# Thirty-two repeated columns in the narrow matmuls of a decode kernel

## The chip, the cores and the metric

The kernel runs on one core of a Trainium2 chip. The metric is device time in microseconds (us) of one execution of the whole program; lower is better. The core's engines are TensorE (PE in the profile; its weight loads are listed apart as PEld), VectorE (DVE), ScalarE (ACT), GpSimd (POOL) and SyncE (SP), which here only issues transfers between the chip's memory (HBM) and the on-chip memory (SBUF). TensorE writes to PSUM, eight banks of 128 partitions by 512 fp32 columns. The profile lists the share of its full clock that TensorE was granted (PEclk).

## The reference

Two layers of attention and gated MLP, one token for each of four sequences, all in bf16. Both layers use the same weights and the same caches.

```python
B, Sq, D = 4, 1, 512;  Hq, Hkv, Sk, Dh = 32, 8, 4096, 128;  F = 1792

def A(x, k_cache, v_cache, wq, wo):
    q = (x @ wq).reshape(B, Sq, Hq, Dh).transpose(0, 2, 1, 3)
    k = jnp.repeat(k_cache, 4, axis=1)
    v = jnp.repeat(v_cache, 4, axis=1)
    scores = jnp.einsum("bhqd,bhkd->bhqk", q, k) * (Dh ** -0.5)
    p = softmax(scores)
    o = jnp.einsum("bhqk,bhkd->bhqd", p, v)
    return o.transpose(0, 2, 1, 3).reshape(B, Sq, Hq * Dh) @ wo

def B_(x, w_gate, w_up, w_down):
    return (sigmoid(x @ w_gate) * (x @ w_up)) @ w_down

for layer in range(2):
    x = x + A(layernorm(x), A_k_cache, A_v_cache, A_wq, A_wo)
    x = x + B_(layernorm(x), B_w_gate, B_w_up, B_w_down)
```

One sequence and one KV head have a K and a V of 4096 x 128, 1 MB each; there are 32 such pairs, read in each layer. Four query heads share a KV head.

## The kernel before

**Units.** A layer has 32 units (one sequence, one KV head). `ORDER` lists pairs of units, 32 pairs over both layers, and the main loop (from L1343) takes one pair at a time: scores, softmax and transpose of pair `sg`, and in the same round the product with V of the pair before it, `vg`.

**Transfers.** SBUF has twelve slots of 1 MB and, after the last use of the query weights, four more in their place. `pump` (L441) issues the next K, V or weight load, in the fixed order of `LOADS`, as soon as a slot is free, all from the SP queue. A slot is free when the matmuls that read it (scores L996, product with V L1154) are done, so a late matmul holds up the load that is to reuse its slot and, in the queue, all loads behind it. `RET` names units whose K or V stays in its slot from layer 0 to layer 1.

**A pair.** VectorE transposes K in its slot in 32 x 32 blocks (`k_turn`, L981). `scores` (L983) issues, for each unit, four rounds of four matmuls; the four of a round have a stationary tile of 128 x 32 each, go to four different strips of 32 columns of the array, and stream 256 columns. The softmax is one row maximum on VectorE, one exponential on ScalarE, and small matmuls that spread the maximum (L1042) and sum the parts (L1090). `ptrans` (L1107) turns P with two matmuls that stream 128 columns (L1112), and 16 copies on ScalarE and VectorE take it to SBUF (L1137, L1131).

**Product with V** (`pv`, L1141; `pv_last`, L1171, for the last pair). V is the stationary operand: for each unit 32 matmuls, each with a 128 x 128 tile of V as weights, stream the 4 columns of P that belong to the four query heads and add into 4 columns of the PSUM bank `O_ps[p]`. `normalise` (L1207) multiplies the 8 columns of a pair by the reciprocal sums.

**Output projection** (`wo_mm`, L1221): 32 matmuls with 128 x 128 tiles of `wo` as weights and 1 or 2 columns (one or two sequences) each, into columns 64 to 71 of the same bank; `wo_add` (L1245) adds them to the residual `xT`.

**A pass.** When all units of a sequence in layer 0 are done, its MLP and its next queries run as 23 steps (`pass_steps`, L943), spread over the rounds of the main loop by the table `PLACES`: layer norm (`ln_a`, `ln_b`), gate and up (`wide`, through `wide_mm`, L798: 56 matmuls each, one streamed column), `gate_tanh`, `gate_mul`, `down` (L918: 56 matmuls, one column) and `down_add`; then a second layer norm and `q_row` (L868), which has one column of weights and streams 512 columns of the query weights, four matmuls at a time in four strips; last `q_turn` and `q_spread`. There are four passes, one for each sequence. Each engine works through its instructions in program order, so the steps of a pass stand in TensorE's queue between the matmuls of the pairs.

**The tail** (from L1460) is the MLP of layer 1 for all four sequences at once: gate and up with 4 streamed columns (`wide_mm` again, 56 matmuls each), then `down_rows` (L1484), which has the hidden state as weights (128 x 32 tiles in four strips) and streams 128 columns of `w_down`.

The weights of gate, up, down, output projection and V are all 128 x 128 tiles that are used once each. Each matmul is preceded by a load of its tile (PEld).

Of the kernel before, what the change touches and what calls it, by code (L numbers as in the profile page):

```python
# [6 lines left out]
ACTF = mybir.ActivationFunctionType  # L7
ALU = mybir.AluOpType
# [236 lines left out]
def bass_interleave_layers__gqa_block_cached__glu_gated_glu__decode_kernel(  # L245
# [12 lines left out]
    Bn, Sq, D = A_x.shape  # L258
    _, HKV, SK, DH = A_k_cache.shape
    HQ = A_wq.shape[1] // DH  # L260
    REP = HQ // HKV
    F = B_w_gate.shape[1]
    P = 128
    assert Sq == 1 and DH == P and D == 512 and F % P == 0 and SK == 4096
    assert REP == 4 and Bn == 4 and HKV == 8
    KD = D // P
    KF = F // P
    NJ = SK // P
    XJ = 4
    JG = NJ // XJ  # L270
    NT4 = 4
    NLAYER = 2
    NSLOT = 12
    eps = 1e-5
# [46 lines left out]
    xT = sbt([P, KD, Bn], dt.float32, "xT")  # L321
# [3 lines left out]
    lnsum, _, vpe, nt_a, nt_b, nt_c, nt_y, rs = [newt[:, i, :] for i in range(8)]  # L325
    y0i = newt[:, 8, :].bitcast(dt.int32)
    xc_bf = sbt([P, KD, Bn], dt.bfloat16, "xc_bf")
# [23 lines left out]
    O_ps = [pst("O_ps0"), pst("O_ps1")]  # L351
# [223 lines left out]
    def head_masks():  # L575
# [44 lines left out]
            writes=["blk"],  # L620
        )

    def bsl(b0, nb):
        return slice(b0, b0 + nb)

# [172 lines left out]
    def wide_mm(nb, which, f0, f1, M, mk):  # L798
        wsb, keys = ((wg_sb, wkeys["wg"]), (wu_sb, wkeys["wu"]))[which]
        fns = []  # L800
        for fc in range(f0, f1):
            for k in range(KD):
                fns.append(
                    (lambda fc, k: lambda e: e.matmul(  # L804
                        M[:, 64 + fc * nb:64 + (fc + 1) * nb],
                        lhsT=wsb[:, k, bass.ds(2 * P * (fc // 2) + fc % 2, P, step=2)],
                        rhs=xc_bf[:, k, 0:nb],
                        start=(k == 0),
                        stop=(k == KD - 1),
                    ))(fc, k)  # L810
                )
        S.group("pe", fns, reads=["xcb"] + keys, writes=[mk])

    def tail_tanh():
        dve(
            lambda e: e.tensor_tensor(
                gs_sb.rearrange("p (k b) -> p k b", k=KF),
                M_ps[0][:, 64:64 + KF * Bn].rearrange("p (k b) -> p k b", k=KF),
                bc(rs[:, 0:Bn], KF, Bn),
                ALU.mult,  # L820
            ),
            reads=["M0", "rs"],
            writes=["pe0"],
        )
        act(
            lambda e: e.activation(t_sb, gs_sb, ACTF.Tanh),
            reads=["pe0"],
            writes=["pe0"],
        )

    def tail_mul(h, f0, f1, M, mk, hk):
        dve(
            lambda e: e.scalar_tensor_tensor(
                out=h[:, f0:f1, :],
                in0=t_sb.rearrange("p (k b) -> p k b", k=KF)[:, f0:f1, :],
                scalar=-1.0,
                in1=M[:, 64 + f0 * Bn:64 + f1 * Bn].rearrange("p (k b) -> p k b", b=Bn),
                op0=ALU.add,
                op1=ALU.mult,
            ),  # L840
            reads=["pe0", mk, "h_w"],
            writes=[hk],
        )
# [7 lines left out]

    def gate_tanh():
        act(
            lambda e: e.activation(th, M_ps[0][:, 64:64 + KF], ACTF.Tanh, scale=rs[:, 0:1]),
            reads=["rs", "M0"],
            writes=["xc"],
        )

    def gate_mul():
        dve(  # L860
            lambda e: e.scalar_tensor_tensor(
                out=hT_bf[:, :, 0], in0=th, scalar=-1.0, in1=M_ps[1][:, 64:64 + KF], op0=ALU.add, op1=ALU.mult
            ),
            reads=["xc", "M1"],
            writes=["qT"],
        )
# [51 lines left out]
    def down(nb, c0):  # L918
        fns = []
        for c in range(c0, c0 + 2):  # L920
            for k in range(KF):
                fns.append(
                    (lambda c, k: lambda e: e.matmul(  # L923
                        M_ps[0][:, 128 + c * nb:128 + (c + 1) * nb],
                        lhsT=wd_sb[:, k, bass.ds(2 * P * (c // 2) + c % 2, P, step=2)],
                        rhs=hT_bf[:, k, 0:nb],
                        start=(k == 0),
                        stop=(k == KF - 1),
                    ))(c, k)
                )  # L930
        S.group("pe", fns, reads=["qT"] + wkeys["wd"], writes=["M0"])

    def down_add(b):
        dve(
            lambda e: e.scalar_tensor_tensor(
                out=xT[:, :, b], in0=M_ps[0][:, 128:128 + KD], scalar=rs[:, 0:1], in1=xT[:, :, b],
                op0=ALU.mult, op1=ALU.add,
            ),
            reads=["M0", "rs"],
            writes=[f"x{b}"],  # L940
        )
# [200 lines left out]
    def pv(i):  # L1142
        l, b, u = seq[i]
        g, ul = divmod(i, 2)
        p = g % 2
        s = where["v", b, u]
        pT = pT_sb[p]
        vv = slot[s].rearrange("p (j d) -> p j d", d=DH)
        for x in range(XJ):
            fns = []  # L1150
            for c in range(4):
                for j in range(2):
                    fns.append(
                        (lambda x, c, j: lambda e: e.matmul(  # L1154
                            O_ps[p][:, ul * REP:(ul + 1) * REP],
                            lhsT=vv[:, x * JG + c * 2 + j, :],
                            rhs=pT[:, x, j, 2 * c + ul, :],
                            start=(x == 0 and c == 0 and j == 0),
                            stop=(x == XJ - 1 and c == 3 and j == 1),
                        ))(x, c, j)  # L1160
                    )
            key = f"pT_{x}"
            rd = [f"s{s}", key] + [f"{key}_{a}" for a in range(3)]
            if ul == 0 and x == 0:
                S.group("pe", fns, reads=rd, writes=[f"O{p}"])
            else:
                S.last_write[f"O{p}"] = S.group("pe", fns, reads=rd)
        if l == 1 or not kept("v", i):
            free.append(where.pop(("v", b, u)))

    def pv_last(g):  # L1171
        p = g % 2
        l, b, u = seq[2 * g]
        ss = [where.pop(("v", b, u + ul)) for ul in range(2)]
        pT = pT_last.rearrange("p (j n a h) -> p j n a h", j=2, a=4, h=REP)
        for ul in range(2):
            vv = slot[ss[ul]].rearrange("p (a s j d) -> p a s j d", a=4, s=4, j=2)
            for a in range(4):
                fns = []
                for s in range(4):  # L1180
                    for j in range(2):
                        fns.append(
                            (lambda ul, vv, a, s, j: lambda e: e.matmul(  # L1183
                                O_ps[p][:, ul * REP:(ul + 1) * REP],
                                lhsT=vv[:, a, s, j, :],
                                rhs=pT[:, j, 2 * s + ul, a, :],
                                start=(a == 0 and s == 0 and j == 0),
                                stop=(a == 3 and s == 3 and j == 1),
                            ))(ul, vv, a, s, j)
                        )  # L1190
                rd = [f"v{ul}_{a}", "q0", "q1"]
                if ul == 0 and a == 0:
                    S.group("pe", fns, reads=rd, writes=[f"O{p}"])
                else:
                    S.last_write[f"O{p}"] = S.group("pe", fns, reads=rd)
        free.extend(ss)
# [10 lines left out]
    def normalise(g):  # L1207
        l, b, u = seq[2 * g]
        p = g % 2
        n, c = oplace(l, b)  # L1210
        assert (n, u, c) not in held, (l, b, u)
        held[n, u, c] = (l, b)
        dve(
            lambda e: e.tensor_tensor(  # L1214
                oT_sb[n][:, u * REP:(u + 2) * REP, c], O_ps[p][:, 0:2 * REP], rden_sb[p], ALU.mult
            ),
            reads=[f"O{p}", f"rden{p}"],
            writes=[f"oT{n}_{u}_{c}"],
        )

    def wo_mm(g, p):  # L1221
# [8 lines left out]
        for c in range(KD):  # L1230
            for r in range(2 * REP):
                fns.append(
                    (lambda c, r: lambda e: e.matmul(  # L1233
                        O_ps[p][:, 64 + 2 * c:64 + 2 * c + nb],
                        lhsT=wo_sb[:, u * REP + r, bass.ds(2 * P * (c // 2) + c % 2, P, step=2)],
                        rhs=oT_sb[n][:, u * REP + r, 0:nb],
                        start=(r == 0),
                        stop=(r == 2 * REP - 1),
                    ))(c, r)
                )  # L1240
# [4 lines left out]
    def wo_add(g, p):  # L1245
# [5 lines left out]
        xs = xT[:, :, bass.ds(b0, nb, step=max(1, b1 - b0))]  # L1251
        dve(
            lambda e: e.tensor_tensor(
                xs, xs, O_ps[p][:, 64:64 + 2 * KD].rearrange("p (k two) -> p k two", two=2)[:, :, 0:nb], ALU.add
            ),
            reads=[f"x{b0}", f"x{b1}", f"O{p}"],
            writes=[f"x{b0}", f"x{b1}"],
# [318 lines left out]
```

## Time and profile before

| | |
|---|---|
| median of 3 runs | 311.92 us (311.75, 311.92, 314.68) |
| span of the profiled execution | 310.4 us |
| median less span | 1.5 us |
| read from HBM | 115.61 MB |
| matmuls | 5268, of which 1984 in L1154, 640 in L1233, 560 in L804, 224 in L923, 64 in L1183 |
| matmuls of the scores (L996) | 1024 |
| matmuls of `q_row` (L874) | 128 |

The total time of the profiled execution is not listed beside its span; the 1.5 us between the span and the median are taken as what lies around it. A matmul counts as busy from its issue until its result is in PSUM. Matmuls overlap, and busy time counts overlapping ones once, so a busy PE had work in flight; how much of its rate that used is not said. In rows of stretches, the columns are: from and to, length, busy us and count for PE, PEld, DVE, ACT and POOL, then the granted share of TensorE's clock, the share of the 16 DMA engines, and GB/s. Rows of one source line have PE and PEld alone. In rows of a timeline the first two numbers are start and length.

### The profile page before, as it was taken

Reading aid. Unit: us, or ns where it says so; the run is one execution under the profiler, and the core shown is the slowest. Engines: PE = TensorE matmul, PEld = TensorE weight load, DVE = VectorE, ACT = ScalarE, POOL = GpSimd, SP = SyncE. Lnnn points to the kernel's source line nnn. Section 1 sums busy time; section 2 is a strip of 40 time slices with the busy share of each in tenths; the row PEclk is TensorE's granted clock in tenths of the full one; section 3 lists DMA queues with packets and bytes.
Section 4 is the critical chain, followed back from the end, with each engine's and each line's share of the span. In section 5 each row is a group of like instructions: output and inputs, shape, how many; then the busy total and the mean of one; then the engine's idle time right before and its main releaser. Section 6 shows DMA issues by size and latency. Waiting matters only on the chain. (4 is left out here: it accounts for less than half of the span.)

```text
span 310.4 us, 12244 instructions
## 1 busy us (share of the span) xinstructions
PE 231.6 (75%) x5268; PEld 160.9 (52%) x5268; DVE 205.9 (66%) x597; ACT 118.9 (38%) x489; POOL 26.0 (8%) x106
## 2 busy tenths in 40 slices
PE   1373565676878967589998684889777869988786
PEld 0331113345664645467756462775555658476586
DVE  4654768988646448875854967576888358458823
ACT  1040241345511544325246655513266542545510
POOL 0000000000000100000011000000110000011200
PEclk9999999995555555555557555556555555557555
DMA  7999999999999999999999999999999998999900
GB/s 294 414 400 414 414 421 420 420 419 417 414 405 353 343 414 423 417 420 367 357 358 354 424 422 420 419 378 390 396 422 419 383 423 290 377 387 424 344 18 3
DMA packets 19169, 116.39 MB, mean 375 GB/s; under 512 B 1960, under 2 KB 1964, under 8 KB 6444
## 3 DMA queue, kind: packets, MB, share of 16 engines
q1 hardware_dynamic: 19116, 115.62, 92.8%
q8 instruction: 41, 0.67, 0.8%
q14 instruction: 12, 0.10, 0.1%
HBM read 115.61 MB, written 0.00 MB: 372 GB/s over the span
## 5 line engine op out<-in xcount | busy, mean ns | idle before, releaser
L981 DVE STREAM_TRANSPOSE slot<-slot 128x1024 f32<-128x1024 f32 (+1 forms) x57 | 98.0, 1726 | 10.5 <-DMA slot<-in_A_k_cache_dram 10.4
L1137 ACT ACTIVATE pT<-PT 32x64 bf16<-32x64 f32 x388 | 83.4, 215 | 40.1 <-PE PT L1112 30.4
L996 PE MATMUL S_ps<-slot,qz 128*32 128x256 bf16 x976 | 61.3, 407 | 22.3 <-DVE slot L981 20.5
L1154 PE MATMUL O_ps<-pT,slot 128*128 128x4 bf16 x1952 | 62.9, 166 | 13.2 <-ACT pT L1137 5.9
L1154 PEld LDWEIGHTS O_ps<-pT,slot 128*128 128x128 bf16 x1952 | 58.2, 104 | 22.0 <-ACT pT L1137 9.8
L996 PEld LDWEIGHTS S_ps<-slot,qz 128*32 128x32 bf16 x976 | 28.7, 128 | 38.0 <-DVE slot L981 20.7
L1067 ACT ACTIVATE pe<-S_ps,small 128x256 bf16<-128x256 f32 x32 | 15.5, 485 | 79.5 <-DVE small L1055 55.0
L1081 POOL TENSOR_TENSOR small<-small 128x1 f32<-128x1 f32 x64 | 12.5, 195 | 240.6 <-ACT pe L1067 238.1
L1131 DVE CAST pT<-PT 32x64 bf16<-32x64 f32 x108 | 24.0, 222 | 6.1 <-PE PT L1112 2.9
L1233 PE MATMUL O_ps<-oT,wo 128*128 128x2 bf16 (+1 forms) x640 | 20.1, 165 | 2.2 <-DVE oT L1214 1.9
L1233 PEld LDWEIGHTS O_ps<-oT,wo 128*128 128x128 bf16 x640 | 18.9, 104 | 4.4 <-DVE oT L1214 4.3
L561 ACT ACTIVATE wo<-M_ps 128x512 bf16<-128x512 f32 x14 | 8.3, 594 | 31.9 <-PE M_ps L551 31.8
L1019 DVE TENSOR_REDUCE small<-S_ps 128x1 f32<-128x256 f32 x32 | 13.2, 411 | 6.7 <-PE S_ps L996 6.4
L551 PE MATMUL M_ps<-wo,row 64*128 64x512 bf16 x56 | 14.1, 599 | 4.1 <-DVE wo L566 2.6
L1214 DVE TENSOR_TENSOR oT<-O_ps,rden 128x8 bf16<-128x8 f32 x32 | 5.0, 155 | 16.5 <-PE O_ps L1154 13.6
L874 PE MATMUL M_ps<-wq,xc_bf 128*1 128x512 bf16 x128 | 15.3, 594 | 0.5
L1112 PE MATMUL PT<-ident_bf,pe 128*128 128x128 bf16 x64 | 12.0, 290 | 4.8 <-ACT pe L1067 4.7
L788 POOL TENSOR_TENSOR qz<-qc,small 128x128 bf16<-128x128 bf16 x32 | 12.6, 401 | 28.9 <-ACT qc L774 28.9
L1042 PE MATMUL MS<-row_max,mask_f 128*128 128x16 bf16 x64 | 6.9, 181 | 10.5 <-DVE row_max L1025 10.5
L566 DVE CAST wo<-M_ps 128x512 bf16<-128x512 f32 x14 | 9.6, 683 | 6.5 <-PE M_ps L551 6.4
L1055 DVE CUSTOM_DVE_ANT_0 junk<-MS,small 128x16 bf16<-128x16 f32 x32 | 6.8, 212 | 9.5 <-PE MS L1042 9.4
L1042 PEld LDWEIGHTS MS<-row_max,mask_f 128*128 128x128 bf16 x64 | 4.1, 107 | 16.6 <-DVE row_max L1025 13.6
(104 smaller groups left out, 205.4 us busy)
## 6 DMA issues: line engine op xcount, KB each, us to landing
slot<-in_A_v_cache_dram SPq DMA_DIRECT2D x49, 1024.0 KB, 10.4
slot<-in_A_k_cache_dram SPq DMA_DIRECT2D x42, 1024.0 KB, 10.2
wq<-in_A_wq_dram SPq DMA_DIRECT2D x4, 1024.0 KB, 7.8
wo<-in_A_wo_dram SPq DMA_DIRECT2D x8, 512.0 KB, 14.4
wq<-in_A_k_cache_dram SPq DMA_DIRECT2D x3, 1024.0 KB, 11.8
slot<-in_A_v_cache_dram SPq DMA_DIRECT2D x8, 256.0 KB, 16.5
wg<-in_B_w_gate_dram SPq DMA_DIRECT2D x2, 896.0 KB, 18.3
wu<-in_B_w_up_dram SPq DMA_DIRECT2D x2, 896.0 KB, 9.9
```

The source lines that it names most:

```text
L551: (lambda h, i, rows: lambda e: e.matmul(ps[h][:, :], lhsT=spread_w[i][rows, :], rhs=wo_sb[rows, c + i, :], start=(i == 0), stop=(i == 1), ...
L788: lambda e: e.tensor_tensor(qz_sb[z][:, :, 0:4 * REP].rearrange("p i (a r) -> p i a r", r=REP), qc_sb[:, b, u:u + 2, :, :].rearrange("p u ...
L874: (lambda k, st: lambda e: e.matmul(M_ps[h][32 * st:32 * st + 1, :], lhsT=xc_bf[:, k, 0:1], rhs=wv[:, k, h, :, st, :], start=(k == 0), sto ...
L981: dve(lambda e: e.transpose(kf, kf), writes=[f"s{st}"])
L996: (lambda t, b2, e_, w0, s: lambda e: e.matmul(S_ps[p][32 * s:32 * s + 8 * REP, 0:2 * P], lhsT=qzf[:, w0:w0 + 8 * REP], rhs=ktv[:, :, s, : ...
L1019: lambda e: e.tensor_reduce(m, S_ps[p][:, 0:2 * P], AX.X, ALU.max),
L1067: lambda e: e.activation(to, frm, ACTF.Exp, bias=nm_sb[p], scale=exp_scale, accum_out=sm_sb[p][0],),
L1081: (lambda n: lambda e: e.tensor_tensor(sm_sb[p][n + 1], sm_sb[p][n], top(sm_sb[p][n]), ALU.subtract))(n),
L1131: (lambda dst, frm: lambda e: e.tensor_copy(dst, frm))(dst, frm),
L1137: (lambda dst, frm: lambda e: e.activation(dst, frm, ACTF.Copy))(dst, frm),
L1154: (lambda x, c, j: lambda e: e.matmul(O_ps[p][:, ul * REP:(ul + 1) * REP], lhsT=vv[:, x * JG + c * 2 + j, :], rhs=pT[:, x, j, 2 * c + ul, ...
L1233: (lambda c, r: lambda e: e.matmul(O_ps[p][:, 64 + 2 * c:64 + 2 * c + nb], lhsT=wo_sb[:, u * REP + r, bass.ds(2 * P * (c // 2) + c % 2, P, ...
```

## The change

The matmuls of five functions get their right-hand operand repeated, so that each streams 32 columns: `wide_in` reads the same 1, 2 or 4 columns 32, 16 or 8 times (a stride of zero, no copy is made), and `wide_out` gives the result 32 columns of PSUM in place of 1, 2 or 4. Every repeat computes the same numbers. `wide_cols` picks the first 1, 2 or 4 of each 32 for the readers. The weights, the number of matmuls and of weight loads, their order, the semaphores and the transfers are as they were. The places in PSUM move: product with V to columns 0 to 63, output projection to 64 to 191, gate and up to 64 to 511, down to 128 to 255 of their banks, and the instructions of VectorE and ScalarE that read them now step by 32 columns.

```diff
+    WIDE = 32
...
+    def wide_in(ap):
+        n = ap.shape[1]
+        return ap.unsqueeze(1).broadcast_to([P, WIDE // n, n])
+
+    def wide_out(M, i, n):
+        return M[:, WIDE * i:WIDE * (i + 1)].rearrange("p (w n) -> p w n", n=n)
+
+    def wide_cols(M, i, k, n):
+        return M[:, WIDE * i:WIDE * (i + k)].rearrange("p (k w) -> p k w", w=WIDE)[:, :, 0:n]
...
# wide_mm (gate and up)
-                        M[:, 64 + fc * nb:64 + (fc + 1) * nb],
+                        wide_out(M, 2 + fc, nb),
                         lhsT=wsb[:, k, bass.ds(2 * P * (fc // 2) + fc % 2, P, step=2)],
-                        rhs=xc_bf[:, k, 0:nb],
+                        rhs=wide_in(xc_bf[:, k, 0:nb]),
...
# gate_tanh
-            lambda e: e.activation(th, M_ps[0][:, 64:64 + KF], ACTF.Tanh, scale=rs[:, 0:1]),
+            lambda e: e.activation(th, wide_cols(M_ps[0], 2, KF, 1)[:, :, 0], ACTF.Tanh, scale=rs[:, 0:1]),
...
# down
-                        M_ps[0][:, 128 + c * nb:128 + (c + 1) * nb],
+                        wide_out(M_ps[0], 4 + c, nb),
                         lhsT=wd_sb[:, k, bass.ds(2 * P * (c // 2) + c % 2, P, step=2)],
-                        rhs=hT_bf[:, k, 0:nb],
+                        rhs=wide_in(hT_bf[:, k, 0:nb]),
...
# pv (pv_last in the same way)
-                            O_ps[p][:, ul * REP:(ul + 1) * REP],
+                            wide_out(O_ps[p], ul, REP),
                             lhsT=vv[:, x * JG + c * 2 + j, :],
-                            rhs=pT[:, x, j, 2 * c + ul, :],
+                            rhs=wide_in(pT[:, x, j, 2 * c + ul, :]),
...
# normalise
-                oT_sb[n][:, u * REP:(u + 2) * REP, c], O_ps[p][:, 0:2 * REP], rden_sb[p], ALU.mult
+                oT_sb[n][:, u * REP:(u + 2) * REP, c].rearrange("p (t r) -> p t r", t=2),
+                wide_cols(O_ps[p], 0, 2, REP),
+                rden_sb[p].rearrange("p (t r) -> p t r", t=2),
+                ALU.mult,
...
# wo_mm
-                        O_ps[p][:, 64 + 2 * c:64 + 2 * c + nb],
+                        wide_out(O_ps[p], 2 + c, nb),
                         lhsT=wo_sb[:, u * REP + r, bass.ds(2 * P * (c // 2) + c % 2, P, step=2)],
-                        rhs=oT_sb[n][:, u * REP + r, 0:nb],
+                        rhs=wide_in(oT_sb[n][:, u * REP + r, 0:nb]),
...
```

The other readers (`tail_tanh`, `tail_mul`, `gate_mul`, `down_add`, `wo_add`) change in the way of `gate_tanh`. The scores, `q_row`, `ptrans`, the layer norms and `down_rows` are not touched.

More of the change, by code (lines that the diff above doesn't have):

```diff
@@ L817, in tail_tanh @@
                 gs_sb.rearrange("p (k b) -> p k b", k=KF),
-                M_ps[0][:, 64:64 + KF * Bn].rearrange("p (k b) -> p k b", k=KF),
+                wide_cols(M_ps[0], 2, KF, Bn),
                 bc(rs[:, 0:Bn], KF, Bn),
@@ L836, in tail_mul @@
                 scalar=-1.0,
-                in1=M[:, 64 + f0 * Bn:64 + f1 * Bn].rearrange("p (k b) -> p k b", b=Bn),
+                in1=wide_cols(M, 2 + f0, f1 - f0, Bn),
                 op0=ALU.add,
@@ L861, in gate_mul @@
             lambda e: e.scalar_tensor_tensor(
-                out=hT_bf[:, :, 0], in0=th, scalar=-1.0, in1=M_ps[1][:, 64:64 + KF], op0=ALU.add, op1=ALU.mult
+                out=hT_bf[:, :, 0], in0=th, scalar=-1.0, in1=wide_cols(M_ps[1], 2, KF, 1)[:, :, 0],
+                op0=ALU.add, op1=ALU.mult,
             ),
@@ L935, in down_add @@
             lambda e: e.scalar_tensor_tensor(
-                out=xT[:, :, b], in0=M_ps[0][:, 128:128 + KD], scalar=rs[:, 0:1], in1=xT[:, :, b],
+                out=xT[:, :, b], in0=wide_cols(M_ps[0], 4, KD, 1)[:, :, 0], scalar=rs[:, 0:1], in1=xT[:, :, b],
                 op0=ALU.mult, op1=ALU.add,
@@ L1183, in pv_last @@
                             (lambda ul, vv, a, s, j: lambda e: e.matmul(
-                                O_ps[p][:, ul * REP:(ul + 1) * REP],
+                                wide_out(O_ps[p], ul, REP),
                                 lhsT=vv[:, a, s, j, :],
-                                rhs=pT[:, j, 2 * s + ul, a, :],
+                                rhs=wide_in(pT[:, j, 2 * s + ul, a, :]),
                                 start=(a == 0 and s == 0 and j == 0),
@@ L1253, in wo_add @@
             lambda e: e.tensor_tensor(
-                xs, xs, O_ps[p][:, 64:64 + 2 * KD].rearrange("p (k two) -> p k two", two=2)[:, :, 0:nb], ALU.add
+                xs, xs, wide_cols(O_ps[p], 2, KD, nb), ALU.add
             ),
```

## The prediction

> **What bounds the kernel now.** I read the page first: the busy shares, then the slices of clock and transfers.
>
> ```profile
> span 310.4 us, 12244 instructions
> ...
> PE 231.6 (75%) x5268; PEld 160.9 (52%) x5268; DVE 205.9 (66%) x597; ACT 118.9 (38%) x489; POOL 26.0 (8%) x106
> ...
> PEclk9999999995555555555557555556555555557555
> DMA  7999999999999999999999999999999998999900
> GB/s 294 414 400 414 414 421 420 420 419 417 414 405 353 343 414 423 417 420 367 357 358 354 424 422 420 419 378 390 396 422 419 383 423 290 377 387 424 344 18 3
> ```
>
> Transfers bound most of the span: many slices stand at about 421 GB/s. But some fall to 343 to 390, and at the end there are none. The waits of the transfer queue say what it waits for; columns are total us, times, longest.
>
> ```profile
> SPq L237 <- PE O_ps L1154: 108.7, 40, 8.1
> SPq L237 <- PE S_ps L996: 64.2, 21, 6.2
> ```
>
> It waits for matmuls that free a slot. While other transfers are in flight such a wait costs nothing; so I cut out the four stretches in which GB/s fell, which hold the four MLP passes, and the tail.
>
> ```profile
> 80.00:112.00 32.00, 26.00 (x595) 18.42 (x592) 16.33 (x65) 10.56 (x45) 2.92 (x12) 0.50 0.97 377
> 144.00:170.00 26.00, 24.59 (x593) 17.66 (x590) 15.62 (x59) 10.57 (x45) 2.28 (x9) 0.56 0.93 347
> 200.00:224.00 24.00, 20.21 (x502) 14.83 (x501) 17.65 (x60) 6.42 (x26) 1.54 (x6) 0.57 0.99 387
> 256.00:280.00 24.00, 22.75 (x535) 16.09 (x531) 14.88 (x60) 10.07 (x43) 2.28 (x9) 0.50 0.93 354
> 296.00:310.40 14.40, 11.30 (x360) 10.62 (x356) 4.60 (x25) 1.13 (x4) 0.00 (x0) 0.50 0.02 5
> ```
>
> There TensorE is busy 94 of 106 us, at a granted clock of 0.50 to 0.57. Against 421 GB/s the four lose 32(1-377/421)=3.3, 4.6, 1.9 and 3.8 us, 13.7 together: what a faster TensorE could win there at most. The 14.4 us of the tail have no transfers. So the clock matters in 120 of 310 us.
>
> **What moves the clock.** These are stretches of 3.41 us, cut where the granted clock changes or might have changed.
>
> ```profile
> 156.49:159.91 3.42, 3.42 (x58) 1.36 (x50) 1.21 (x8) 1.35 (x4) 0.39 (x2) 0.50 0.96 383
> 159.91:163.32 3.41, 3.06 (x102) 2.71 (x101) 1.95 (x7) 1.07 (x5) 0.76 (x2) 0.50 0.89 320
> ...
> 211.10:214.52 3.42, 3.35 (x43) 0.84 (x35) 2.96 (x16) 1.69 (x9) 0.00 (x0) 0.50 1.01 371
> 214.52:217.93 3.41, 2.82 (x86) 2.02 (x82) 1.86 (x9) 1.15 (x3) 0.39 (x2) 1.00 1.01 423
> ...
> 296.43:299.84 3.41, 3.37 (x128) 3.30 (x124) 0.88 (x4) 0.38 (x1) 0.00 (x0) 0.50 0.02 5
> 299.84:303.26 3.42, 3.10 (x77) 2.80 (x73) 0.94 (x6) 0.51 (x2) 0.00 (x0) 0.50 0.02 5
> ```
>
> All three upper rows of the pairs are full of matmuls, yet only the second is followed by a clock of 1.00, which lasts one such stretch. The timeline shows the difference and, further down, what the clock is worth.
>
> ```profile
> 24.24 1.05 PE L996 MATMUL S_ps<-slot,qz 128*32 128x256 bf16 x16 [2.45 <-DVE slot L981]
> 105.75 0.30 PE L763 MATMUL M_ps<-qT,ident_bf 128*32 128x32 bf16 x16
> 156.23 1.88 PE L874 MATMUL M_ps<-wq,xc_bf 128*1 128x512 bf16 x16
> 159.03 1.02 PE L874 MATMUL M_ps<-wq,xc_bf 128*1 128x512 bf16 x8
> 211.95 2.84 PE L874 MATMUL M_ps<-wq,xc_bf 128*1 128x512 bf16 x24
> 244.12 1.01 PE L1154 MATMUL O_ps<-pT,slot 128*128 128x4 bf16 x32
> 245.00 0.37 PE L1112 MATMUL PT<-ident_bf,pe 128*128 128x128 bf16 x2
> 245.30 1.04 PE L996 MATMUL S_ps<-slot,qz 128*32 128x256 bf16 x16
> 283.37 0.94 PE L1154 MATMUL O_ps<-pT,wq 128*128 128x4 bf16 x32
> 285.19 0.65 PE L996 MATMUL S_ps<-wq,qz 128*32 128x256 bf16 x16 [0.29 <-DVE oT L1214]
> 297.17 1.85 PE L1183 MATMUL O_ps<-slot,slot 128*128 128x4 bf16 x64
> 298.88 2.03 PE L1233 MATMUL O_ps<-oT,wo 128*128 128x2 bf16 x64
> 306.05 1.45 PEld L1489 LDWEIGHTS PT<-wd,slot 128*32 128x32 bf16 x56 [0.15 <-issue]
> 306.08 1.68 PE L1489 MATMUL PT<-wd,slot 128*32 128x128 bf16 x56
> ```
>
> The rate first. L1489 runs 14 rounds of four strips, 128 columns each; less a last matmul of 0.31 us (the form's mean, below) 13 rounds take 1.37 us, 105 ns each: 1.2 columns per ns, or 0.83 ns per column, at clock 0.50. Now the columns streamed. From 211.10: six rounds of 512 (2.56 us) and the end of 16 score matmuls from 210.80, some 0.5 us: about 0.9 of the stretch. From 156.49: 1.45 us left of four rounds, then two, 0.85 us: 0.70. From 296.43: some 95 matmuls of 2 or 4 columns every 27 ns: 0.1. So columns streaming through the array raise the clock and loading weights does not, from a share between 0.70 and 0.9; I take 0.75 as an estimate. One warning: the 1.00 of the first 67 us is no measurement. Sixteen score matmuls take 1.05 us at 24.24, as at 245.30 with 0.50, but 0.65 at 285.19, with a true 1.00. The profile's mean clock is too high by that.
>
> **The change part by part.** Weights, order, waits and transfers stay. Three things change.
>
> First, the added columns. A narrow matmul comes every (1.01-0.17)/31 = 27 ns at clock 0.50, with 0.17 from the first row here.
>
> ```profile
> L1154 PE MATMUL O_ps<-pT,slot 128*128 128x4 bf16 x1952 | 62.9, 166 | 13.2 <-ACT pT L1137 5.9 <-issue 3.9 <-DMA slot<-in_A_v_cache_dram 3.2
> L1489 PE MATMUL PT<-wd,slot 128*32 128x128 bf16 x56 | 1.7, 311 | 0.1
> ```
>
> One or four columns make no difference to it (L1233 with 2: (2.03-0.17)/63 = 30 ns, with a wait in it), so the load of 128 columns sets the 27 ns. The new stream is 32 x 0.83 = 27 ns: it just fits, if load and stream run at once. Rows for that: the two L1112, full tiles with 128 columns, take 0.37 us. One takes 0.17 and 124 more columns of 0.83 ns, 0.27; the second stream adds 0.107: 0.376. Nothing is left for a second load of 27 ns, which would give 0.40. L763, 32 columns behind loads of 32, is the form nearest in size: four rounds in 0.30, less one matmul of some 0.19 (0.17 and 28 columns), leaves 0.11 for three, 37 ns at most, its start included. So 0 to 10 ns more for each narrow matmul; I take 0, by L1112, which has the same full tile. [...]
>
> Second, latency. The last matmul of each group ends 28 columns later, 23 ns at 0.50. Where a pair's work fills the wait it costs nothing. On the chain of a pass there are five such ends (product with V, projection, gate, up, down), and five in the tail: 25 x 0.023 = 0.6 us, taken as if nothing hid it. The readers in PSUM touch as many elements as before, with another step: 0.
>
> Third, the clock. I work it out for the stretch from 144 to 170. Its lines by source, PE and PEld, in this order: L996, L874, L1154, L804, L923, L1233.
>
> ```profile
> 144.00:170.00 26.00, 5.86 (x100) 0.56 0.93 347
> 144.00:170.00 26.00, 3.92 (x32) 0.56 0.93 347
> 144.00:170.00 26.00, 5.88 (x192) 0.56 0.93 347
> 144.00:170.00 26.00, 3.58 (x112) 0.56 0.93 347
> 144.00:170.00 26.00, 1.81 (x56) 0.56 0.93 347
> 144.00:170.00 26.00, 1.35 (x45) 0.56 0.93 347
> ```
>
> Streamed at 0.83 ns per column: scores 25 rounds of 256, 5.3 us; queries 8 rounds of 512, 3.4; the 405 narrow ones about 1. That is 0.37 of 26 us. With 32 columns the narrow ones stream 10.8 us: 0.75. The mean now stands at the threshold, so about half of the 3.41 us stretches should pass it. As the row from 214.52 shows, a rise lasts one stretch when the next streams little (there 82 narrow matmuls and few others). A rise after every second or third stretch makes 0.33 to 0.5 of the time; I take 0.4. Already granted are 0.12 and 0.14 in the second and third stretch, 0.065 on the mean of four: net 0.335.
>
> What full clock saves in that stretch: scores 1.04 to 0.65 for 16, so 6.25 x 0.39 = 2.4 us; queries half of 3.4, 1.7; narrow matmuls (1.01-0.94)/31 = 2 ns each, 405 of them, 0.8. Together 4.9 us in 26, or 0.19 us per us. By the number of matmuls (595+593+502+535 = 2225 against 593) the four stretches would save 18.4 us at full clock, and 18.4 x 0.335 = 6.2 at the share above. How much of that brings transfers forward? None where a slot was free in time; all where the queue stood. TensorE is busy in 0.88 of these stretches, but a saving in front of a wait on VectorE is lost. I take two thirds, 4.1 us, well under the 13.7. The bounds are 0 and 6.2. In the 190 us outside, transfers run at 421 GB/s and cover TensorE: 0.
>
> The tail: the stretch from 296.43 would stream 0.93 instead of 0.1, so the next, from 299.84, has full clock; then one without, then full clock from 306.67, inside L1489, which halves the last 1.1 us of that line: 0.5 saved. For 299.84 to 303.26 I use 0.19 x 3.4 = 0.6. Together 1.1 us.
>
> Sum: -4.1 -1.1 +0.6 = -4.6, a span of 305.8. The median stands 1.5 us above the span: **307.3 us**. With the conversion at 0 it is 311.4, with all of 6.2 it is 305.2.
>
> **The rivals.** *The clock stays up.* The fall after 217.93 came from a stretch with PE busy 2.82 of 3.41 us, but one of mostly narrow matmuls that stream little; wide ones might hold the clock. With a share of 0.8 in the stretches: 18.4 x (0.8-0.065) x 2/3 = 9.0; tail 12 us x 0.19 = 2.3; plus 0.6: a span of 299.7, time 301.2. [...]
>
> *Nothing comes of it.* The clock rises, but the queue is then held by the VectorE chains of the layer norm or the K transposes (DVE busy 17.65 of 24 in the third stretch); or repeats count less than I think. Time 311 to 312.5. For it: shares of 0.75 lie just at the threshold.
>
> *Load and stream do not overlap.* This ends slower. Its place is every narrow matmul of the four stretches and the tail: 2225 x 405/593 = 1520, and 64+64+112 = 240. At 27 ns each it is 47.5 us, a time near 359 with no rise of the clock to set against it, down to 336 if idle time takes half of it. It decides from 4.6/1760 = 2.6 ns per matmul, where it eats the gain; with (4.6+3.1)/1760 = 4.4 ns the kernel is 1% slower. The upper end of 10 ns from L763 would cost 17.6 less 4.6: 325. Against it stands L1112.
>
> *Latency alone*: the clock does not rise, and the ends cost more than 23 ns each because readers queue behind them on in-order engines: 314 to 316.
>
> **Chances.** Forecast 0.50 (own range 304.5 to 310); clock stays up 0.12; nothing 0.22; no overlap 0.10; latency alone 0.06. One per cent, 308.8 and 315.0, is about what a measurement of this kernel tells from no change (three runs spread over 311.75 to 314.68). Of the forecast's half, 0.40 lies below 308.8 and 0.10 above; with 0.12 for a held clock that is 0.52 faster. Same: 0.10, 0.22 and 0.04 of latency, 0.36. Slower: 0.12. The range runs from 301, which takes in the held clock at its worked-out size, to 312.5, which takes in the nothing case. Outside lie the slower two, 0.16, and some 0.04 for a clock that gives more than worked out.
>
> **What would show it.** In the profile after: 32 matmuls of L1154 still in 1.0 us at clock 0.50; granted stretches of 1.00 in each pass and from about 299.8; GB/s over 365 in the four stretches, later ones starting earlier; scores at 0.65 us for 16 in more places. A spacing of 54 ns, or a clock that stays 0.50 while 0.8 of a stretch streams, would prove the first or third step wrong; a risen clock with unchanged GB/s, the conversion.

## The result, and the profile after

| | before | after |
|---|---|---|
| median, first comparison | 311.84 us (4 runs) | 307.89 us (4 runs) |
| ratio, with its 95% interval | | 0.9856 (0.9809 to 0.9903) |
| ratio in two repeats on other occasions | | 0.9912 (0.9883 to 0.9940), 0.9894 (0.9851 to 0.9938) |
| span of the profiled execution | 310.4 us | 306.0 us |

The three intervals together put the gain at about 1%, some 3 us; the forecast was 4.6 us and 307.3 us. The medians of the two repeats were 309.19 beside 311.88 us and 308.80 beside 312.60 us, so the forecast lies a little under all three. The ratios leave out executions in the chip's slower state and the medians do not, so the two can differ by some tenths of a per cent.

The page of the changed kernel, first its span, busy time, granted clock and transfer rate in 40 slices:

```profile
span 306.0 us, 12244 instructions
...
PE 221.0 (72%) x5268; PEld 157.6 (51%) x5268; DVE 206.1 (67%) x597; ACT 118.2 (39%) x489; POOL 25.8 (8%) x106
...
PEclk9999997956655797565799777575965575879567
...
GB/s 289 415 398 413 417 420 419 422 417 420 415 401 356 359 420 423 416 418 391 357 386 381 424 423 417 419 422 388 356 423 420 384 379 347 334 418 420 399 93 3
```

TensorE's busy time fell by 10.6 us though its 3472 narrow matmuls stream 32 columns each; the clock line has many slices over 5 where it had few. Next, the four stretches of the passes, cut at the same times as before (columns as in the prediction):

```profile
80.00:112.00 32.00, 25.84 (x617) 18.91 (x613) 16.54 (x65) 10.59 (x46) 2.75 (x12) 0.66 0.98 384
144.00:170.00 26.00, 20.97 (x603) 16.59 (x602) 18.40 (x60) 11.47 (x49) 2.27 (x9) 0.89 0.98 372
200.00:224.00 24.00, 18.59 (x460) 13.03 (x458) 16.55 (x54) 5.52 (x23) 1.53 (x6) 0.77 0.98 389
256.00:280.00 24.00, 21.47 (x590) 16.57 (x587) 17.15 (x66) 9.75 (x42) 2.26 (x9) 0.80 0.95 369
```

In all four the clock rose. The rates are 377 to 384, 347 to 372, 387 to 389 and 354 to 369 GB/s; against 421 GB/s these four lose 2.8, 3.0, 1.8 and 3.0 us, 10.6 where it was 13.7. Only the second of these differences stands out from what executions differ by: 342 to 351 GB/s in the four runs below that have a clock of at most 0.64 there (places alone, 16 columns, 24 columns, added work), 357 to 377 in the four other traces with 32 columns. In the third and fourth stretch the kernel with the new places alone, nearly at the old clock, has rates above those of the changed kernel:

```profile
200.00:224.00 24.00, 20.16 (x485) 14.08 (x486) 17.52 (x58) 5.75 (x23) 1.53 (x6) 0.57 1.00 409
256.00:280.00 24.00, 22.59 (x538) 15.79 (x537) 15.75 (x63) 9.96 (x42) 2.26 (x9) 0.57 0.98 375
```

Near the end of the loads, both kernels in steps of 2 us, before first:

```profile
292.00:294.00 2.00, 2.00 (x53) 1.45 (x53) 1.58 (x7) 1.41 (x7) 0.00 (x0) 0.50 0.90 326
294.00:296.00 2.00, 0.99 (x34) 0.91 (x33) 0.53 (x4) 0.83 (x2) 0.39 (x2) 0.50 0.29 106
```

```profile
290.00:292.00 2.00, 1.76 (x61) 1.65 (x58) 1.21 (x7) 0.50 (x1) 0.00 (x0) 0.50 0.96 353
292.00:294.00 2.00, 1.95 (x68) 1.85 (x64) 0.67 (x3) 0.72 (x3) 0.39 (x2) 0.50 0.35 128
```

The loads end some 2 us earlier. The timeline gives the rest, each row with its start and length; the first two show the stream's fit, the last two the tail:

```profile
151.54 0.95 PE L1166 MATMUL O_ps<-pT,slot 128*128 128x32 bf16 x32
...
152.77 0.66 PE L1008 MATMUL S_ps<-slot,qz 128*32 128x256 bf16 x16
...
292.59 1.06 PE L1166 MATMUL O_ps<-pT,slot 128*128 128x32 bf16 x32
...
293.57 1.87 PE L1195 MATMUL O_ps<-slot,slot 128*128 128x32 bf16 x64
295.27 1.83 PE L1248 MATMUL O_ps<-oT,wo 128*128 128x32 bf16 x64
```

The last product with V starts at 293.57, where it started at 297.17 before: 3.6 us earlier. From there to the end it is 306.0-293.57 = 12.4 us, before 310.4-297.17 = 13.2: 0.8 us. Together that is the 4.4 us between the spans. Executions of the kernel before lie anywhere from 309.8 to 314.4 us on three occasions, and an experiment below with nearly the old clock has a span of 308.4, so a split read from one execution of each is good to a us or two.

### The profile page after: what moved, and what is told of

It reads as the page before. It is cut to its first block, busy times and chain, and to the rows that moved or that the text cites. A ratio compares the mean times of both kernels' runs of the same rounds, so it can differ in the third digit from the quotient of the medians.

```text
span 306.0 us, 12244 instructions
## 1 busy us (share of the span) xinstructions
PE 221.0 (72%) x5268; PEld 157.6 (51%) x5268; DVE 206.1 (67%) x597; ACT 118.2 (39%) x489; POOL 25.8 (8%) x106
## 5 line engine op out<-in xcount | busy, mean ns | idle before, releaser
L1166 PE MATMUL O_ps<-pT,slot 128*128 128x32 bf16 x1952 | 63.0, 183 | 11.5 <-ACT pT L1149 4.7
L1008 PE MATMUL S_ps<-slot,qz 128*32 128x256 bf16 x976 | 53.4, 363 | 22.6 <-DVE slot L993 19.2
L1166 PEld LDWEIGHTS O_ps<-pT,slot 128*128 128x128 bf16 x1952 | 56.9, 101 | 19.8 <-ACT pT L1149 8.6
L1079 ACT ACTIVATE pe<-S_ps,small 128x256 bf16<-128x256 f32 x32 | 15.5, 484 | 77.0 <-DVE small L1067 34.4
L1008 PEld LDWEIGHTS S_ps<-slot,qz 128*32 128x32 bf16 x976 | 26.0, 116 | 36.0 <-DVE slot L993 19.4
L1093 POOL TENSOR_TENSOR small<-small 128x1 f32<-128x1 f32 x64 | 12.4, 193 | 236.6 <-ACT pe L1079 234.1
L1248 PE MATMUL O_ps<-oT,wo 128*128 128x32 bf16 x640 | 21.3, 187 | 4.6 <-issue 2.2
L1054 PE MATMUL MS<-row_max,mask_f 128*128 128x16 bf16 x64 | 6.9, 178 | 14.8 <-DVE row_max L1037 14.5
L1031 DVE TENSOR_REDUCE small<-S_ps 128x1 f32<-128x256 f32 x32 | 13.2, 411 | 5.0 <-PE S_ps L1008 4.6
L552 PE MATMUL M_ps<-wo,row 64*128 64x512 bf16 x56 | 13.3, 565 | 4.1 <-DVE wo L567 2.6
L1124 PE MATMUL PT<-ident_bf,pe 128*128 128x128 bf16 x64 | 11.1, 270 | 4.3 <-ACT pe L1079 4.1
L886 PE MATMUL M_ps<-wq,xc_bf 128*1 128x512 bf16 x128 | 12.0, 478 | 0.5
```

The costliest lines, as they stand in the source:

```text
L552: (lambda h, i, rows: lambda e: e.matmul(ps[h][:, :], lhsT=spread_w[i][rows, :], rhs=wo_sb[rows, c + i, :], start=(i == 0), stop=(i == 1), ...
L886: (lambda k, st: lambda e: e.matmul(M_ps[h][32 * st:32 * st + 1, :], lhsT=xc_bf[:, k, 0:1], rhs=wv[:, k, h, :, st, :], start=(k == 0), sto ...
L1008: (lambda t, b2, e_, w0, s: lambda e: e.matmul(S_ps[p][32 * s:32 * s + 8 * REP, 0:2 * P], lhsT=qzf[:, w0:w0 + 8 * REP], rhs=ktv[:, :, s, : ...
L1031: lambda e: e.tensor_reduce(m, S_ps[p][:, 0:2 * P], AX.X, ALU.max),
L1079: lambda e: e.activation(to, frm, ACTF.Exp, bias=nm_sb[p], scale=exp_scale, accum_out=sm_sb[p][0],),
L1093: (lambda n: lambda e: e.tensor_tensor(sm_sb[p][n + 1], sm_sb[p][n], top(sm_sb[p][n]), ALU.subtract))(n),
```

## The experiments

**Theory.** Columns that stream through the array raise the granted clock when they fill about three quarters of a stretch of 3.41 us. The share is the prediction's estimate, between a stretch of 0.70 without a rise after it and one of 0.9 with one; the length is that of the trace, for the 8 and 36 clock records of the kernels before and after all start a whole number of 3.41 us from the first of their trace. 32 repeats lift the passes over that mark at next to no cost, because the loads of weights hide them (32 products with V take 1.06 us at half clock from 292.59, 1.01 before); the faster TensorE frees slots sooner (the loads end some 2 us earlier). **Rivals.** The new places in PSUM do it; one part of the matmuls does it alone; any repeat counts; or, the clock being right, more clock would give more. All ratios are against the kernel before, run beside it. The page's mean clock isn't compared between kernels, since all slices ahead of the first recorded change read 9.

**Places alone, 16 columns, 24 columns.** The helpers get a width; the places stay.

```diff
-    def wide_in(ap):
+    def wide_in(ap, w=WIDE):
         n = ap.shape[1]
-        return ap.unsqueeze(1).broadcast_to([P, WIDE // n, n])
+        return ap.unsqueeze(1).broadcast_to([P, w // n, n])
...
# places alone: w = n at every call; 16 and 24 columns: w = 16, w = 24 at every call
```

Expected of the places alone:

> The PSUM places and readers of the changed kernel, but 1 to 4 streamed columns as before. Theory (time comes from the clock, the clock from streamed columns): four single stretches of 3.41 us at full clock as before, mean clock 0.63, time 311.0 to 312.6. Rival (the new places or stepped readers give the gain, or cost something): 308 or over 313 at an unchanged clock.

Expected of 16 columns:

> 16 streamed columns in place of 32, everywhere. Theory: share from 144 to 170 of 0.37 + 0.38/2 = 0.56, below the threshold of about 0.75 in most stretches of 3.41 us, so a mean clock of 0.63 to 0.68 and a time of 310 to 312. Rival (any repeat counts, or matmul busy time counts): clock 0.72 to 0.75 and 307 to 308.5. If the 29 to 31 ns of gate and down come from the stream not quite fitting, they go back to 27.

Expected of 24 columns:

> 24 streamed columns in place of 32. Theory (a threshold near 0.75 of a stretch of 3.41 us): the share from 144 to 170 is 0.37 + 0.75 x 0.38 = 0.66, so more rises than with 16 columns (7) and fewer than with 32 (16 to 18), full clock for 40 to 80 us in all, time between 309.5 and 311.5. Rival (any stream above 16 columns does it): 16 or more rises, 100 us or more, and the time of the changed kernel.

Measured: places alone 0.9994 (0.9968 to 1.0020); 16 columns 1.0018 (0.9990 to 1.0046); 24 columns 0.9972 (0.9937 to 1.0006). The clock line of each page, in this order, one fence for each kernel:

```profile
PEclk9995555555555755555556555555655555575555
```

```profile
PEclk9999999996555575575567555556555555557555
```

```profile
PEclk9999999995555765575578775555755665557556
```

A 5 is half clock. After the leading nines (no record yet) there are 5, 7 and 13 rises in the three traces, 18 in the changed kernel (16 in each of its two repeats); full clock lasts 17, 24 and 48 us, against 106 (109 and 99). So the places and the stepped readers do nothing to the time, 16 columns nothing, and 24 nothing that can be told from none. A threshold would fit that: of the 13 rises that 32 columns add to the 5 of the places alone, half of the columns add 2, and none of the gain. Rises and full clock of 24 columns are as expected. The expected time of 16 columns (310 to 312) was met as a ratio; its median of 313.1 us was not.

**One part alone.** The product with V wide and the rest narrow, and the reverse.

```diff
# product with V alone: in wide_mm, down and wo_mm
-                        wide_out(M, 2 + fc, nb),
+                        wide_out(M, 2 + fc, nb, nb),
...
-                        rhs=wide_in(xc_bf[:, k, 0:nb]),
+                        rhs=wide_in(xc_bf[:, k, 0:nb], nb),
...
# the rest alone: in pv and pv_last
-                            wide_out(O_ps[p], ul, REP),
+                            wide_out(O_ps[p], ul, REP, REP),
```

Expected of the product with V alone:

> 32 columns in the product with V alone; gate, up, down and output projection stream 1 to 4. Theory: from 144 to 170 the streamed share falls from 0.75 to (5.3+3.4+192 x 0.027)/26 = 0.53, so clock there under 0.75 where the changed kernel has 0.89, and in the tail no rise after the output projection; time 309 to 310.5. Rival (the product with V, the most numerous, gives all): 307.5 to 308.5.

Expected of the rest alone:

> 32 columns in gate, up, down and output projection alone; the product with V streams 4. Theory: share from 144 to 170 of (5.3+3.4+0.6+213 x 0.027)/26 = 0.58, clock there under 0.75, outside the passes 0.50; time 309 to 310.5. Rival (only the narrow matmuls of the passes matter, since the transfers cover the rest): 307.5 to 308.5. Spacing of gate and down 29 to 31 ns as in the changed kernel.

Measured: 0.9968 (0.9934 to 1.0002) and 0.9998 (0.9963 to 1.0032), medians 311.85 and 311.70 us beside 311.75. The clocks were as expected, under 0.75 in every stretch; here the second, for V alone and then for the rest:

```profile
144.00:170.00 26.00, 22.43 (x575) 16.16 (x573) 17.42 (x60) 11.53 (x50) 2.26 (x9) 0.68 0.96 351
```

```profile
144.00:170.00 26.00, 24.44 (x616) 18.03 (x609) 16.25 (x61) 11.33 (x49) 2.28 (x9) 0.70 0.96 356
```

The times missed: I expected 309 to 310.5 of both. Neither part gains anything that can be told from none, and the two ratios together would make 0.3%; both at once make 1%. Rates stay at 351 and 356 GB/s at a clock near 0.7, and reach 372 only at 0.89. But the rest alone has 10 rises and 34 us of full clock, and V alone has 16 rises and 78 us, three quarters of the changed kernel's:

```profile
PEclk9995557956555855575569575755757765598575
```

So the sum of full clock does not give the time by itself. In the four stretches V alone has 0.61, 0.68, 0.62 and 0.72; by the prediction's 18.4 us and the conversion found below that would be worth about 1.5 us, which its interval (up to 2.1 us) does not exclude. These runs do not settle whether V alone gains that or nothing.

**No single column repeated.** In the changed kernel a trait showed that I had not forecast: down, with one column repeated 32 times, takes 2.09 us for 56 matmuls at full clock, where the product with V takes 0.95 for 32. Single columns were written 2 or 4 times side by side and those repeated.

```diff
-                out=hT_bf[:, :, 0], in0=th, scalar=-1.0, in1=wide_cols(M_ps[1], 2, KF, 1)[:, :, 0],
+                out=hT_bf[:, :, 0:Bn], in0=th.unsqueeze(2).broadcast_to([P, KF, Bn]), scalar=-1.0, in1=wide_cols(M_ps[1], 2, KF, Bn),
...
-                        rhs=wide_in(hT_bf[:, k, 0:nb]),
+                        rhs=wide_in(hT_bf[:, k, 0:Bn]),
...
# the same for xc_bf (4 copies) and for oT of single sequences (2 copies)
```

Expected:

> The changed kernel with 2 or 4 copies of the one streamed column written side by side, so that no matmul repeats a single column (gate, up, down and projection of single sequences: 928 matmuls, spacing 30 ns against 27 in the product with V, and 30 at full clock against 25). Theory (a column repeated with stride zero is read more slowly): spacing back to 27 at half clock and 25 at full; 928 x 3 to 5 ns = 3 to 4.5 us of TensorE's time, two thirds of it in the end: 2 to 3 us under the changed kernel. Rival (the 30 ns come from the weights' stride of 2 or from the bank): spacing unchanged, time the same as the changed kernel.

Measured: 0.9907 (0.9884 to 0.9930), beside 0.9912 for the changed kernel on the same chip. Down in the timeline, changed kernel and then copies, both at full clock:

```profile
149.61 2.09 PE L935 MATMUL M_ps<-qT,wd 128*128 128x32 bf16 x56
```

```profile
150.03 1.80 PE L936 MATMUL M_ps<-qT,wd 128*128 128x32 bf16 x56
```

Over all starts in the trace the spacing of a repeated single column is 30 to 31 ns at half and at full clock; with copies it is 27.0 to 27.3 and 25.0 to 25.6. With 16 repeats of a single column, in the run above, it was 27.0 to 27.3 at half clock, as 16 columns read at the same slow pace, some 15 ns (an estimate, half of the 30 to 31 for 32), would still fit beside the load's 27 ns. So the theory of the cause holds, and what it should have given, 2 to 3 us, did not come. Once more, beside another run of the changed kernel:

> The changed kernel again, to be compared with the next two on one chip: 0.985 to 0.992 of the kernel before.

> The kernel with side by side copies again. Theory after the first run (what it saves lies where TensorE then waits for VectorE or for transfers): the same as the changed kernel within 1 us. Rival (the 3 us of TensorE's time count by two thirds): 2 us faster than the changed kernel.

Measured: 0.9894 (0.9851 to 0.9938) and 0.9901 (0.9867 to 0.9935), both as expected. The 3 us of TensorE's time are worth nothing that can be measured.

**More clock.** 64 columns in the product with V, the rest as in the changed kernel (the output projection moves on to columns 128 to 255), which ran again beside it and the next.

```diff
+    def pv_in(ap):
+        return ap.unsqueeze(1).broadcast_to([P, 64 // REP, REP])
+
+    def pv_out(M, i):
+        return M[:, 64 * i:64 * (i + 1)].rearrange("p (w n) -> p w n", n=REP)
...
-                            wide_out(O_ps[p], ul, REP),
+                            pv_out(O_ps[p], ul),
...
-                            rhs=wide_in(pT[:, x, j, 2 * c + ul, :]),
+                            rhs=pv_in(pT[:, x, j, 2 * c + ul, :]),
```

Expected of the changed kernel again, and of 64 columns:

> The changed kernel once more, on the chip of the next three, so that they can be compared with it. Theory and rival alike: 0.98 to 0.99 of the kernel before, clock in the four stretches 0.65 to 0.9.

> 64 streamed columns in the product with V, 32 in the rest. Theory: 53 ns spacing at half clock, 27 at full; stretches of product with V always pass the threshold, so a clock of 0.8 to 0.95 in the four stretches; what that wins is set against 1984 x 27 ns x the half-clock share (about 0.25): within 1.5 us of the changed kernel. Rival (a clock that is up nearly always wins more): 301 to 304.

Measured: 0.9912 (0.9883 to 0.9940), just outside what was expected, and 1.0027 (0.9990 to 1.0064). The clock line of 64 columns, and the same product at half clock and at full:

```profile
PEclk9999997979956759976699979669969798999799
```

```profile
95.82 1.87 PE L1172 MATMUL O_ps<-pT,slot 128*128 128x64 bf16 x32
...
156.75 1.09 PE L1172 MATMUL O_ps<-pT,slot 128*128 128x64 bf16 x32
```

Full clock lasted 184 us, the most of all, and the gain is gone: at half clock 32 products take 1.87 us in place of 1.06, and at full clock 1.09 in place of 0.95. My forecast missed too: by the two ratios the kernel is 3.6 us slower than the changed kernel, where I expected 1.5 us at most. The rival that more clock wins more falls, at this price; what so much clock would win without the price is not shown. The run also shows what the forecast's slower rival would have looked like: at half clock the 1.87 us, less a last matmul of some 0.22 (0.17 and 60 columns of 0.83 ns), leave 53 ns for each of 31, the 64 x 0.83 ns of the stream and no longer the 27 ns of the load.

**What TensorE's time is worth.** The kernel before, with 9 more narrow matmuls in each product with V of the main loop.

```diff
+            for c in range(3 if x < XJ - 1 else 0):
+                fns.append(
+                    (lambda x, c: lambda e: e.matmul(
+                        O_ps[p][:, 400:404],
+                        lhsT=vv[:, x * JG + c, :],
+                        rhs=pT[:, x, 0, c, :],
+                        start=False,
+                        stop=False,
+                    ))(x, c)
+                )
```

Expected:

> The kernel before with 9 more narrow matmuls in each product with V (4 columns, into PSUM columns that nobody reads): 558 x 27 ns = 15 us of TensorE's time, 209 of them, 5.6 us, in the four stretches, and no change of the clock. It measures what TensorE's time is worth in the end. Theory (two thirds of the time in the four stretches reaches the end): 3.7 us slower than before. Rival (transfers cover it): within 1 us of before. If all of it counted: 15 us slower.

Measured: 1.0273 (1.0238 to 1.0307), 8.5 us for 15 us of work. That lies between my 3.7 and all of it, and above the theory. Part of the reason is in a stretch that I had counted as covered by transfers, before and then with the added work:

```profile
224.00:256.00 32.00, 24.75 (x574) 17.54 (x578) 22.01 (x52) 17.78 (x80) 3.70 (x15) 0.50 1.01 413
```

```profile
224.00:256.00 32.00, 25.45 (x634) 18.65 (x630) 23.60 (x54) 16.12 (x72) 3.12 (x13) 0.50 0.98 373
```

The cover there is thin: with more work for TensorE the rate fell from 413 to 373 GB/s, though by then the run is 4 to 6 us late, and the stretch holds the end of the third pass as well. Counted by the starts of the same matmuls in both traces, the work of 224 to 256 lost 1.9 us of the 8.8 between the spans. The work of the four stretches lost 4.4 us, for 5.6 us added there; so two thirds were too low inside the stretches too. Here, time added to TensorE ahead of the release of a slot cost more than time taken from it brought.

## Why the prediction was right

**What bounds it.** Right in direction, and shown in part. Counted by the starts of the same matmuls, the five traces with 32 columns (three of the changed kernel, two with copies) gain 0.5 to 1.3 us on the kernel before in the work of 80 to 112, and 0.7 to 1.3 us from the last product with V to the end; places alone, 16 and 24 columns gain -1.1 to 0.3 and -0.2 to 0.2. In between the lead moves up and down by up to 2.8 us, in those three kernels by up to 2.1, so the rest of the gain cannot be put to one stretch. That all 190 us outside run at 421 GB/s was misread: the row from 224 has 413, and from 280 to 296 it is 363.

**The added columns cost nothing.** Right for the product with V: 32 matmuls take 1.06 us at half clock, less one of 0.19 (row below) 28 ns each, and 0.95 at full. By all starts it is 27.1 and 25.4 ns. The rival that load and stream do not overlap, with its 54 ns (27 of load and 27 of stream), is refuted by these rows. Wrong for one column repeated: 3 to 5 ns more, inside the 0 to 10 that the prediction kept as bounds, and without effect on the time.

**Latency.** Right: the mean of one narrow matmul in the last product with V, which runs at half clock in both kernels, went from 166 (the prediction's L1154 row has the same form) to 188 ns, 22 where 23 were forecast. What the 25 ends cost together, 0.6 us in the forecast, was not measured apart.

```profile
L1195 PE MATMUL O_ps<-slot,slot 128*128 128x32 bf16 x64 | 1.9, 188 | 0.0
```

**The clock.** Right in kind: full clock lasted 106 us with 32 columns and 17 with the places alone. The size was too small. By the granted clock, 0.66, 0.89, 0.77 and 0.80, full clock filled 0.32, 0.78, 0.54 and 0.60 of the four stretches, 0.55 over their 106 us, where I took 0.40 (0.49 and 0.47 in the two repeats). The step that failed is that a rise lasts one stretch of 3.41 us. In the second pass it lasted six, and seven in both repeats; the row before the rise, then three of the six:

```profile
146.00:149.42 3.42, 3.36 (x106) 2.98 (x102) 3.01 (x5) 0.27 (x1) 0.00 (x0) 0.50 0.93 338
149.42:152.83 3.41, 3.35 (x104) 2.94 (x100) 2.59 (x8) 0.56 (x2) 0.39 (x2) 1.00 1.00 372
152.83:156.24 3.41, 2.56 (x46) 1.04 (x45) 2.94 (x17) 2.93 (x13) 0.00 (x0) 1.00 1.00 377
...
166.49:169.90 3.41, 0.89 (x30) 0.82 (x31) 3.38 (x4) 2.42 (x12) 0.00 (x0) 1.00 1.01 418
```

So the rival of a held clock was right in part. It did not reach its 301 us, and in the run with 64 columns holding the clock by longer streams did not pay (184 us of full clock, a ratio of 1.0027).

**The conversion.** This term was too large. That it nearly cancels the error in the clock is luck: 4.1 us were forecast ahead of the tail, 3.6 came. With a net share of 0.55-0.065 = 0.485 TensorE saves 18.4 x 0.485 = 8.9 us in the stretches by my own rate. The last product with V started 3.6 us earlier: 0.4 of it at most, not two thirds. In the first repeat it started 2.4 us earlier, 0.3 of the 7.8 us by the same sum. Outside the stretches the clock rose too, to 0.56 to 0.67 from 112 to 296, so the whole saving was larger still. Where some of the rest went is seen from 166.49 to 169.90: full clock, transfers at 418 GB/s, VectorE busy 3.38 of 3.41 us and TensorE 0.89. In the whole stretch from 144 to 170 TensorE's idle time rose from 26-24.59 = 1.4 to 26-20.97 = 5.0 us. Over the run its longest single cause that grew is the wait for the row maximum; TensorE's waits, before and after:

```profile
PE MS L1042 <- DVE row_max L1025: 10.5, 12, 1.9
```

```profile
PE MS L1054 <- DVE row_max L1037: 14.5, 14, 2.4
```

The other traces bear it out: 13.7 to 15.5 us in the four others with 32 columns, 10.1 to 10.7 with places alone, 16 and 24 columns. It also fits the copies: in their two traces TensorE is busy 214.6 and 216.6 us, less than in the three of the changed kernel (219.1 to 222.5), and the wait for the row maximum is 15.5 and 13.7 us. That the added work costs 0.57 of itself, while the saved work brings about 0.4 or less, suggests that TensorE, VectorE and the transfers are all near the bound here; it is not shown, for the two kinds of work do not stand in the same places. The 0 for the time outside the stretches did not hold for additions; whether it held for savings the traces do not tell.

**The tail.** 1.1 us were forecast, 0.8 measured. The rises came as worked out, one stretch of full clock, one of half, then full:

```profile
292.79:296.20 3.41, 3.41 (x134) 3.41 (x131) 0.88 (x4) 0.38 (x1) 0.10 (x1) 0.50 0.07 23
296.20:299.61 3.41, 2.98 (x96) 2.67 (x93) 1.45 (x9) 0.51 (x2) 0.00 (x0) 1.00 0.02 5
299.61:303.02 3.41, 3.30 (x128) 3.22 (x128) 1.92 (x12) 0.25 (x1) 0.00 (x0) 0.50 0.02 5
303.02:306.00 2.98, 0.33 (x20) 0.15 (x11) 0.35 (x1) 0.00 (x0) 0.00 (x0) 1.00 0.01 1
```

but the last one met only the end of `down_rows`, since the records of the clock stay a whole number of 3.41 us apart (all 36 of this trace, from 47.02 to 306.44) and the tail had moved by 3.6 us.

**What stays open.** Whether a rise of the clock during the second pass alone, or in one other place, makes most of the gain was not tried. Nor was a kernel in which the row maximum is quicker, which by the waits above should let more of the saved time through. That the gain comes by way of the clock rests on the runs that lack it, and on matmuls that at half clock are no faster than before (32 products with V 1.06 us, 1.01 before); no run raised the clock without wider streams.

## What to carry to other kernels

Here a TensorE that was busy for 75% of the span, much of it with weight loads and narrow streams, had full clock for 13.7 of the 242.7 us from its first clock record on: compare the time of one fixed matmul group at different granted clocks before trusting a busy share (16 score matmuls took 1.05 us at half clock and 0.65 at full), and trust the mean clock not at all where no change is recorded yet. Repeating columns until the stream was as long as the load beside it, 27 ns each, brought 106 us of full clock here at next to no cost (1.06 us for 32 products in place of 1.01); 16 columns brought 24, where the places alone had 17, and 64 set the spacing, 53 ns at half clock. Then price the saved time by an experiment with a little added work and by what waits next, because some of it turned into waits for another engine here (for the row maximum 14.5 us in place of 10.5).

## What was not expected of the hardware

In the changed kernel one column repeated 32 times with a stride of zero takes 30 to 31 ns, at half and at full clock, where in the kernel with copies 2 or 4 columns side by side repeated to 32 take 27 and 25.

Once up, the clock stayed with less streaming than raised it. This was counted over the stretches of 3.41 us of all thirteen traces, from 75 us on, by the starts of the matmuls and at 0.83 ns per column at half clock (the prediction's L1489) and 0.42 at full, where in the changed kernel rounds of 512 columns of `q_row` start 215 ns apart (four matmuls in four strips count as one). The 130 stretches at half clock before a rise streamed 0.63 or more of their time, all but 9 of them 0.72 or more. The 511 without a rise after them streamed up to 0.82, all but 28 of them under 0.72. So the prediction's 0.75 was a fair middle and no sharp line; in the kernel before, the rise at 166.73 follows a stretch that streamed 0.66. At full clock the 113 stretches that kept it streamed 0.35 or more, and the 126 that lost it 0.36 or less.
